# A fifth attention visit with float32 softmax weights, in an instruction order planned from new cost figures

## The chip, the cores and the metric

The kernel runs on one core of one Trainium2 chip. The metric is the device time of one execution in microseconds (us). Three executions of the kernel before took 832.07, 832.44 and 832.96 us; the median is 832.44 us.

## The reference

Hash-bucketed attention for 4 batches of 8 heads, 768 positions of 64 values each, then a two-layer network over the 3072 positions:

```
q_bits, k_bits = (q @ proj > 0), (k @ proj > 0)           # 6 bits: a bucket of 64
mask    = q_bucket == k_bucket
scores  = where(mask, q @ k.T / 8, -1e9)
attn    = softmax(scores)                                  # exp, sum, divide
x       = (attn @ v), heads side by side: 3072 x 512
h       = relu(x @ w_in)                                   # 512 -> 2048
out     = (h * h) @ w_out                                  # 2048 -> 512
```

Everything is float32 at the edges. The kernel gets float32 accuracy from float16 operands by carrying a high and a low half of each number and summing three products.

## The kernel before, in words

**Visits and units.** Attention is cut into 32 visits: one batch, one pair of heads, one half (384) of the queries. A visit has six units: 128 queries of one head against all 768 keys. Batch 0 is visited half by half (`WHOLE`): visits 0 to 3 are the four head pairs on half 0, visits 4 to 7 the same pairs on half 1. The other batches alternate halves pair by pair.

**A unit** (`unit`, L739): TensorE (PE) makes scores into a PSUM tile `pS` in four matmuls, `pS<-A,Q` and `pS<-L,M`; VectorE (DVE) scales them into `e` and finds the maximum; ScalarE (ACT) takes the exponential with its sum; `rv` is the reciprocal of that sum. From here there are two ways:

- the usual way: ACT writes `hl<-e,rv`, the high float16 half of the weights, DVE writes the low half, and SyncE (SP) issues one DMA transpose `aT<-hl`;
- the plain way (`PLAIN_AV`, visits 0 to 3): GpSimd (POOL) multiplies `e` by `rv` in float32, PE transposes it in six pieces `pT`, and ACT or DVE copies each group of three into `aT`. The units below 24 (`EARLY`) use the PSUM tiles `pm` and `pA` for this in turn, later ones a single tile, `misc`.

**The value product of a visit** (`av`, L783) is 36 pairwise float16 matmuls `pA<-aT,VV` the usual way, after V was split into halves, and 12 float32 ones `pA<-aT,V` the plain way, with V as loaded. ACT and DVE then write `xx`, two float16 halves.

**The network** (`moe`, L807) runs in eight stages, one per batch and half, when the four `xx` of that half are there. A stage has 16 steps: 12 matmuls `pm<-xx,win` of 384 columns; ACT and DVE make `g` from them (relu, square, high half, low half); then 9 matmuls `po<-wo,g` of 512 columns, three for each of the three 128-row blocks t. At the end of a stage ACT copies each block out, `o<-po`, and SP stores it. The three blocks lie in three banks of one PSUM tile `po`. The weights `win` and `wo` are split into halves from raw loads in the first fifth of the run: `top<-raw` on ACT, `f<-raw,top` on DVE, `win<-f` and `wo<-f`.

**Checks.** Near the end, `verify` (L882) reads q, k and v again (`X`) and the weights, and makes one flag; a general version of the program stands behind it and is not run with this input.

**What sets the order.** Nothing is issued in the order of the source. `Program.add` records every operation with its dependencies and a cost (`cost`, L195); `forward` (L318) lists them engine by engine against a model of the queues; `backward` refines the priorities; `emit` issues the best order found. So a change of a cost figure moves instructions on all five engines. Each engine then runs its list strictly in that order on the chip. `PACE` ties network steps to units so that PE has network matmuls to run while the attention units wait for the other engines. `region` (L156) says which part of a tile an operation touches: for PSUM it gave single banks, and it held two reads of one bank in order as well.

Of the kernel before, what the change touches and what calls it, by code (L numbers as in the profile page):

```python
# [23 lines left out]
P = 128  # L24
B, H, S, D = 4, 8, 768, 64
NB = 6
HS = 384
# [26 lines left out]
PLAIN_AV, DIVIDE = (0, 1, 2, 3), ("pool",)  # L54

WHOLE = {0: 0}

# [6 lines left out]
RUN = 18  # L64
CONSTS_BY, WIDE = ("sp", "sp", "sp"), 1
# [16 lines left out]
TRANSPOSES = 165  # L82
# [47 lines left out]
class Program:  # L130
# [25 lines left out]
    def region(view):  # L156
# [5 lines left out]
        if rec.kind == "psum":  # L162
            return 0, 1, f0 // 512, 1 + (f0 % rec.row + size(ap.ap[1:]) - 1) // 512, 0, 0, 0
# [5 lines left out]
    def add(self, *ways):  # L169
# [10 lines left out]
        for rec, w, (p0, p1, f0, f1, fs, g0, g1) in used:  # L180
            if rec.before is not None:
                deps |= rec.before.ops
            for j, w2, (a0, a1, b0, b1, bs, c0, c1) in rec.accesses:
                if (w or w2 or rec.kind == "psum") and a0 < p1 and p0 < a1 and b0 < f1 and f0 < b1 and not (fs and fs == bs and (c1 <= g0 or g1 <= c0)):
                    deps.add(j)
# [9 lines left out]
    def cost(key, name, args, kw):  # L195
# [16 lines left out]
        if name.startswith("dma"):  # L212
# [3 lines left out]
            return busy, b / (TRANSPOSES if name == "dma_start_transpose" else 314)  # L216
        if key == "act":
            t = 93 * (isinstance(kw.get("scale"), View) + isinstance(kw.get("bias"), View)) + (51 if "psum" in kinds[:2] else 93) + n / 1.2 + 93 * ("accum_out" in kw)
        elif key == "pool":
            t = 147 + n * (2.1 if args[0].dtype == F32 or args[0].dtype == F32R else 1.88) if name == "tensor_tensor" else 161 + n / 1.2 + 83 * ptr  # L220
        else:
            fast = name in ("tensor_copy", "tensor_scalar") and "psum" not in kinds[:2]
            both = len(args) > 3 and isinstance(args[3], View) and args[3].shape[-1] == 1
            t = 67 + 100 * ("accum_out" in kw) + n / (1.92 if fast else 0.96) + 62 * (ptr and (fast or name == "scalar_tensor_tensor")) + 100 * both
# [93 lines left out]
    def forward(self, prio, near):  # L318
# [7 lines left out]
        free = dict.fromkeys(keys, 0.0)  # L326
        out, dma, dge, held, kind = [], 0.0, 0.0, 0.0, None
# [11 lines left out]
        while True:  # L339
# [21 lines left out]
            if way[5] and held > t and (ready[k] or later[k] and later[k][0][0] < held):  # L361
                heapq.heappush(later[k], (held, i))
                continue
            ends = {}
# [84 lines left out]
def run(ctx: ExitStack, tc, kq, v, proj2, w_in, w_out, consts, out, flag):  # L449
# [56 lines left out]
    if fast:  # L506
# [8 lines left out]
        codes = sb([P, 4 * P], BF16, "codes")  # L515
# [148 lines left out]
    def first(hp):  # L664

        K, G = [sb([P, n], F32, name, tag="VV") for name, n in (("K", S), ("G", HS))]
# [3 lines left out]
        MK, MG = sb([P, S], F16, "MK", tag="M"), sb([P, HS], F16, "MG", tag="Q")  # L670
        halves = K[:, 0:HS], K[:, HS:], G
        pd = ps([P, 512], F32, "pd", tag="misc")[:, 0:HS]
        matmuls(*[(pd[32 * n : 32 * n + 32], pj, x) for n, x in enumerate(halves)])
        bits = sb([P, HS], BF16, "bits")
        act.activation(bits[0:96], pd[0:96], AF.Sign, scale=2.0**60, bias=thr[0:96])
        pc = ps([P, 3, 512], F32, "pc", tag="po")[:, :, 0:HS]
        for n in range(3):
            pe.matmul(pc[:, n], codes[0:96, n * P : (n + 1) * P], bits[0:96], start=True, stop=True)
        for n in range(2):
            dve.tensor_scalar(MK[:, n * HS : (n + 1) * HS], pc[:, n], 3 * 2.0**16, -65504.0, ALU.subtract, ALU.max)  # L680
        pr.add((act, "activation", (MG, pc[:, 2], AF.Relu), {"bias": shift}), (dve, "tensor_scalar", (MG, pc[:, 2], 2.0**16, 0.0, ALU.subtract, ALU.max), {}))
        return K, G, MK, MG

    def side_by_side(st, half, i):

        K, G, MK, MG = st
        c0 = half * HS + i * P
# [51 lines left out]
    def unit(st, half, i, aT, plain, pS=None):  # L739
        c0 = half * HS + i * P  # L740
# [42 lines left out]
    def av(b, hp, half, VV, aTs):  # L783
        pA = ps([P, 512], F32, "pA")[:, 0:HS]
# [8 lines left out]
        xx = xxs[b, half, hp] = sb([P, 2, HS], F16, "xx")  # L793
# [13 lines left out]
    def moe(n, b, half):  # L807
        X = [xxs.pop((b, half, cc)) for cc in range(NCC)]
# [5 lines left out]
        for f in range(NF + 1):  # L814
            if f == NF // 2:
                pr.checked = len(pr.ops)
            if f < NF:
# [3 lines left out]
                for cc in reversed(range(NCC)):  # L821
                    pr.mark = pace()
                    wh = win[:, 0, cc, f * P : (f + 1) * P]
                    wl = win[:, 1, cc, f * P : (f + 1) * P]
                    pe.matmul(pm[:, 0:HS], wh, X[cc][:, 0], start=cc == NCC - 1, stop=False)
                    pe.matmul(pm[:, 0:HS], wh, X[cc][:, 1], start=False, stop=False)
                    pe.matmul(pm[:, 0:HS], wl, X[cc][:, 0], start=False, stop=cc == 0)
                pr.rank, pr.mark = RANK_MOE, None

                g32 = sb([P, HS], F32, "g32", 2)  # L830
                pr.add((act, "activation", (g32, pm[:, 0:HS], AF.Relu), {"scale": HS2 if fast else 2.0**-23}),
                       (dve, "tensor_scalar", (g32, pm[:, 0:HS], HS2 if fast else 2.0**-23, 0.0, ALU.mult, ALU.max), {}))
                square(g32, g32)
                g = gs[f] = sb([P, 2, HS], F16, "g")
# [3 lines left out]
            if f > 0:  # L838
# [4 lines left out]
                if first:  # L843
                    po = ps([P, 3, DM], F32, "po")
                for t in range(3):
# [3 lines left out]
                    pe.matmul(po[:, t], gh, wo[:, 0, m], start=first, stop=False)  # L849
                    pe.matmul(po[:, t], gh, wo[:, 1, m], start=False, stop=False)  # L850
                    pe.matmul(po[:, t], gl, wo[:, 0, m], start=False, stop=last)
# [6 lines left out]
                for t in range(3):  # L858
                    r0 = b * S + half * HS + t * P
# [173 lines left out]
```

## Time and profile before

| | |
|---|---|
| median of three executions | 832.44 us |
| the profiled execution | 834.86 us, of which the span of instructions is 833.1 us |
| PE busy | 794.3 us (95%) |
| ACT busy | 656.6 us (79%) |
| DVE busy | 605.2 us (73%) |
| POOL busy | 72.7 us (9%) |
| DMA queue | 77.2% of 16 engines over the span, 144.93 MB |
| idle filler matmuls at the start | 67 |

A busy PE in this table counts matmuls from start to modelled end, and they overlap, so a stretch in which PE is called busy can still hold lost time. The useful reading is by stage: how much of a stretch PE idles, and what ended the idle time. A stage of the network is easy to find in the trace: its steps repeat `pm` and `po`.

### The profile page before, as it was taken

To read this page: it belongs to the slowest core of one execution; us is meant where nothing else is said; L and a number is where in the kernel's file an instruction comes from. 1 tells how busy PE (TensorE), PEld (TensorE's weight loads), DVE (VectorE), ACT (ScalarE), POOL (GpSimd) and SP (SyncE) were. 2 spreads that over 40 slices of the span, in tenths; PEclk is the share of its full clock that TensorE was granted. 3 is DMA by queue.
4 is the path that set the end of the run, shared out by engine and by line. 5 is a ranking of instruction groups with operands and counts; after the bars stand their busy time and mean duration, and the time that the engine had idled before them with its cause. 6 is when DMAs were issued, how large, how long until landed. Compare 5 with 4: busy or idle time off the path is not lost. (4 is left out here: it accounts for less than half of the span.)

```text
span 833.1 us, 14383 instructions
## 1 busy us (share of the span) xinstructions
PE 794.3 (95%) x5001; PEld 430.0 (52%) x5001; DVE 605.2 (73%) x1200; ACT 656.6 (79%) x1238; POOL 72.7 (9%) x175
## 2 busy tenths in 40 slices
PE   7797799999999999999999999999999999999996
PEld 4354355555555554555555545555555554555553
DVE  6888989998999888898879755888889433611110
ACT  5898999998888989888898856888988997334443
POOL 1255200100000010000000000000002000000000
PEclk9999999999999999999999999999999999999999
DMA  8985979999999999999989866988975889501001
GB/s 258 270 223 181 292 188 179 214 176 195 183 202 196 195 188 213 192 181 219 194 188 186 212 165 140 181 143 148 146 133 99 239 290 304 212 1 39 1 1 42
DMA packets 299521, 145.93 MB, mean 175 GB/s; under 512 B 268752, under 2 KB 279344, under 8 KB 299440
## 3 DMA queue, kind: packets, MB, share of 16 engines
q1 hardware_dynamic: 299440, 144.93, 77.2%
q8 instruction: 41, 0.67, 0.3%
q14 instruction: 40, 0.33, 0.1%
HBM read 56.80 MB, written 6.29 MB: 76 GB/s over the span
## 5 line engine op out<-in xcount | busy, mean ns | idle before, releaser
L427 PE MATMUL po<-wo,g 128*128 128x512 f16 x1152 | 296.9, 379 | 5.7 <-ACT o L427 5.7
L427 PE MATMUL pm<-xx,win 128*128 128x384 f16 x1536 | 297.7, 326 | 4.4 <-ACT g L427 2.8
L427 PEld LDWEIGHTS <-win 128*128 128x128 f16 x1536 | 149.9, 98 | 116.6 <-issue 8.0
L427 DVE TENSOR_SCALAR_CACHE_REDUCE e<-pS 128x768 f32<-128x768 f32 x192 | 182.7, 953 | 21.9 <-PE pS L427 17.7
L427 ACT ACTIVATE e<-e,maxes 128x768 f32<-128x768 f32 x192 | 178.2, 929 | 20.7 <-DVE e L427 19.2
L427 DVE SCALAR_TENSOR_TENSOR hl<-e,rv,hl 128x768 f16<-128x768 f32 x168 | 171.0, 1019 | 18.8 <-ACT hl L427 17.8
L427 PEld LDWEIGHTS <-g 128*128 128x128 f16 x1152 | 111.9, 98 | 124.8 <-issue 9.1
L427 ACT ACTIVATE hl<-e,rv 128x768 f16<-128x768 f32 x168 | 154.6, 923 | 6.0 <-DMA aT<-hl 5.2
L427 DVE SCALAR_TENSOR_TENSOR g<-g,g 128x384 f16<-128x384 f32 x121 | 66.9, 553 | 111.8 <-ACT g L427 111.4
L427 ACT ACTIVATE g<-g 128x384 f32<-128x384 f32 (+1 forms) x251 | 129.4, 517 | 6.6 <-PE po L427 2.7
L427 ACT ACTIVATE g<-pm 128x384 f32<-128x384 f32 x127 | 61.2, 482 | 90.3 <-PE pm L427 90.0
L427 PE MATMUL pS<-A,Q 128*128 128x384 f16 x372 | 93.1, 330 | 4.1 <-DVE e L427 2.6
L427 PE MATMUL pS<-L,M 128*128 128x384 f16 x372 | 91.8, 327 | 0.8 <-DMA M<-Q 0.8
L424 PE MATMUL pA<-aT,VV 128*64 128x384 f16 x1008 | 87.2, 327 | 0.0
L427 POOL TENSOR_SCALAR rv<-sums 128x1 f32<-128x1 f32 x136 | 36.8, 271 | 541.7 <-ACT e L427 400.2
L424 PEld LDWEIGHTS <-VV 128*64 128x64 f16 x1008 | 54.7, 110 | 32.9 <-issue 10.0
L427 PEld LDWEIGHTS <-Q 128*128 128x128 f16 x372 | 34.2, 98 | 43.1 <-issue 16.2
L427 DVE TENSOR_SCALAR M<-pc,masks 128x384 f16<-128x384 f32 x64 | 43.0, 672 | 15.4 <-PE pc L427 15.2
L427 PEld LDWEIGHTS <-M 128*128 128x128 f16 x372 | 36.3, 98 | 25.1 <-DMA M<-Q 1.2
L427 ACT ACTIVATION_READ_ACCUMULATOR e<-e,maxes 128x1 f32 x192 | 36.6, 191 | 0.0
L427 DVE SCALAR_TENSOR_TENSOR L<-R,A 128x768 f16<-128x768 f32 x32 | 30.4, 950 | 7.7 <-ACT A L427 7.5
L427 PE MATMUL pT<-unit_f,e 128*128 128x128 f32 x144 | 23.8, 293 | 10.5 <-ACT aT L427 7.7
(82 smaller groups left out, 517.4 us busy)
## 6 DMA issues: line engine op xcount, KB each, us to landing
R<-kq SPq DMA_DIRECT2D x32, 384.0 KB, 3.8
X<-kq SPq DMA_DIRECT2D x32, 384.0 KB, 4.1
raw<-w_in SPq DMA_DIRECT2D x16, 511.8 KB, 5.6
raw<-w_out SPq DMA_DIRECT2D x16, 511.8 KB, 4.9
V<-vp SPq DMA_DIRECT2D x20, 384.0 KB, 5.1
out<-o SPq DMA_DIRECT2D x24, 256.0 KB, 2.7
X<-vp SPq DMA_DIRECT2D x16, 384.0 KB, 4.4
Q<-L SPq DMA_DIRECT2D x32, 96.0 KB, 2.9
```

The source lines that it names most:

```text
L424: ins = q.engine.matmul(*map(real, args), **kw).ins
L427: ins = getattr(q.engine, o.name)(*map(real, o.args), **{k: real(x) for k, x in o.kw.items()}).ins
```

## The change

Five things are changed together.

1. `PLAIN_AV` gets a fifth visit, visit 4 (batch 0, first head pair, half 1). Its V is the float32 one that visit 0 loaded.
2. The cost figures of the planner are refitted: DMA loads, transposes, their landing and the time that the queue is held; a limit of eight transfers in flight (`LANES`) and of the backlog (`AT_MOST`); faster copies on DVE; slower strided copies on ACT; cheaper side-by-side matmuls.
3. `region` treats a PSUM tile as one piece, and two reads of it are no longer held in order in the plan.
4. In the last stage of the network the three blocks are not in `po`: t = 0 and 1 lie in the scores' tile `pS`, t = 2 in `pA`. In every stage the copy-out of t = 1 goes to DVE.
5. `codes` shares a buffer with `g32`, and half sizes become parameters, with the same values.

```diff
-PLAIN_AV, DIVIDE = (0, 1, 2, 3), ("pool",)
+PLAIN_AV, DIVIDE = (0, 1, 2, 3, 4), ("pool",)
-TRANSPOSES = 165
+TRANSPOSES, INSIDE, LOADING = 190, 230, 325
+SETUP, LANDING, TURNED, HOLD = 100, 1350, 500, 150
+AT_MOST = 2500
+LANES = 8
...
         if rec.kind == "psum":
-            return 0, 1, f0 // 512, 1 + (f0 % rec.row + size(ap.ap[1:]) - 1) // 512, 0, 0, 0
+            return 0, 1, 0, 1, 0, 0, 0
...
-                if (w or w2 or rec.kind == "psum") and a0 < p1 and ...
+                if (w or w2) and a0 < p1 and ...
...
+                if k != "pool":
+                    lanes.append(t + done)
+                    if len(lanes) >= LANES:
+                        busy = max(busy, lanes[-LANES] + 60 - t)
...
                 if first:
-                    po = ps([P, 3, DM], F32, "po")
+                    if fast and (b, q0 + nq) == (B - 1, S):
+                        po = ps([P, 2, 512], F32, "pS"), ps([P, 512], F32, "pA")
+                        po = [po[0][:, 0], po[0][:, 1], po[1]]
+                    else:
+                        po = ps([P, 3, DM], F32, "po")
+                        po = [po[:, t] for t in range(3)]
...
-                        move(o, po[:, t], back)
+                        move(o, po[t], back, (dve,) if fast and t == 1 else (act, dve, pool))
```

Three places in the new order matter for the prediction. The first is PE's list at the very end of the program, with the semaphores that a row waits for. Before:

```order
L427 MATMUL po<-wo,g 128x512
L427 LDWEIGHTS g
L427 MATMUL po<-wo,g 128x512 [waits Activation_49]
L427 LDWEIGHTS g
L427 MATMUL po<-wo,g 128x512
L427 LDWEIGHTS g
L427 MATMUL po<-wo,g 128x512
L427 LDWEIGHTS g
L427 MATMUL po<-wo,g 128x512 [waits Activation_49]
L427 LDWEIGHTS g
L427 MATMUL po<-wo,g 128x512
```

Now:

```order
L445 MATMUL pS<-wo,g 128x512
L445 LDWEIGHTS g
L445 MATMUL pA<-wo,g 128x512
L445 LDWEIGHTS g
L445 MATMUL pA<-wo,g 128x512
L445 LDWEIGHTS g
L445 MATMUL pA<-wo,g 128x512
L445 LDWEIGHTS g
L445 MATMUL pA<-wo,g 128x512
L445 LDWEIGHTS g
L445 MATMUL pA<-wo,g 128x512
```

The two waits for ScalarE between the last five matmuls are gone. Over the whole program 14 `po` rows waited for ScalarE before, at the ends and the starts of stages; in the new order six first rows of stages 2 to 7 wait for an engine that copies out, and none inside a stage. Between the last `po` row of stages 1 to 6 and that waiting row stand 57, 25, 17, 56, 15 and 16 other matmuls; the last stage's first rows wait for no copy-out.

The second place is ACT's list up to the fourth `xx<-pA`, the last input of the first network stage. `top`, `win` and `wo` are the splitting of weights, `aT` and `e,sums` belong to units. Before:

```order
L427 ACTIVATE top_87<-raw 128x512
L427 ACTIVATE aT<-pT 128x3x128 x2
L427 ACTIVATE wo<-f 128x512
L427 ACTIVATE aT<-pT 128x3x128
L427 ACTIVATE e,sums<-e,maxes 128x768
L427 ACTIVATE top_84<-raw 128x512
L427 ACTIVATE wo<-f 128x512
L427 ACTIVATE e,sums<-e,maxes 128x768
L427 ACTIVATE top_87<-raw 128x512
L427 ACTIVATE win<-f 128x512 x2
L427 ACTIVATE xx<-pA 128x384
```

Now:

```order
L445 ACTIVATE top_86<-raw 128x512
L445 ACTIVATE aT<-pT 128x3x128 x2
L445 ACTIVATE e,sums<-e,maxes 128x768
L445 ACTIVATE top_83<-raw 128x512
L445 ACTIVATE aT<-pT 128x3x128
L445 ACTIVATE e,sums<-e,maxes 128x768
L445 ACTIVATE top_86<-raw 128x512
L445 ACTIVATE win<-f 128x512
L445 ACTIVATE e,sums<-e,maxes 128x768
L445 ACTIVATE wo<-f 128x512
L445 ACTIVATE xx<-pA 128x384
```

Counted from the start of the program to that `xx` row, ACT's list had 22 `top`, 13 `win`, 8 `wo`, 26 `e,sums`, 46 `aT`, 7 `A` and 2 `VV` operations, and now has 17, 11, 4, 28, 49, 8 and 1. Weight splitting moved behind it, unit work in front of it. Further on, up to the exponential of the first unit of visit 7, ACT's list had 46 `aT`, 9 `A`, 5 `bits`, 32 `g`, 16 `hl`, 32 `top`, 15 `win`, 16 `wo` and 6 `xx` operations, and now has 60, 12, 6, 29, 11, 31, 12, 13 and 5.

The third place is PE's list where the first network matmuls stand. `pA<-aT,V` is the value product of visit 3, `pT` are float32 transposes. Before:

```order
L427 MATMUL pS<-L,M 128x384
L424 MATMUL pA<-aT,V 64x384 x12
L427 LDWEIGHTS win
L427 MATMUL pm<-xx,win 128x384
L427 LDWEIGHTS Q
L427 MATMUL pS<-A,Q 128x384
L427 LDWEIGHTS Q
L427 MATMUL pS<-A,Q 128x384
```

Now:

```order
L445 MATMUL pS<-L,M 128x384
L445 LDWEIGHTS win
L445 MATMUL pm<-xx,win 128x384
L445 MATMUL pT<-unit_f,e 128x128 x3
L445 LDWEIGHTS win
L445 MATMUL pm<-xx,win 128x384
L445 LDWEIGHTS win
L445 MATMUL pm<-xx,win 128x384
```

The transposes of visit 4 now stand between network matmuls, in groups of three. Before the first `pm` row PE's list holds 46 instead of 42 each of `pS<-A,Q` and `pS<-L,M` (two more units) and 150 instead of 144 transposes; the other 30 transposes of visit 4 come after it.

One count from farther on is used as well. Between the last scores of visit 20 and its value product PE's list had 36 `pm`, 27 `po`, 24 `pS`, 36 `pA<-aT,VV` and 2 `pc` matmuls; now it has 24 `pm`, 26 `po`, 24 `pS`, 4 `pd` and 1 `pc`. Visits 10, 17 and 18 changed in the same way, most other visits less. The 32 squares of `X` on ACT stood behind the `g<-pm` of network steps 88 to 95 of 128; now they stand behind those of steps 95 to 106, seven of them in a row at the first, where stage 7 begins.

More of the change, by code (lines that the diff above doesn't have):

```diff
@@ L325, in forward @@
         ready = {k: [] for k in keys}
-        free = dict.fromkeys(keys, 0.0)
-        out, dma, dge, held, kind = [], 0.0, 0.0, 0.0, None
+        free = dict.fromkeys(keys, 750.0)
+        out, rings, dge, held, kind, lanes = [], [0.0, 0.0], 0.0, 0.0, None, []
         def offer(i):
@@ L363, in forward @@
                 continue
+            if way[1].startswith("dma") and rings[int(k == "pool")] > t + AT_MOST:
+                heapq.heappush(later[k], (rings[int(k == "pool")] - AT_MOST, i))
+                continue
             ends = {}
@@ L736, in values, with unit @@
         return VV
-    def unit(st, half, i, aT, plain, pS=None):
-        c0 = half * HS + i * P
+    def unit(st, c0, i, aT, plain, pS=None):
         u = pr.rank
@@ L805, in unscaled, with moe @@
         return back
-    def moe(n, b, half):
-        X = [xxs.pop((b, half, cc)) for cc in range(NCC)]
+    def moe(n, b, q0, nq):
+        X = [xxs.pop((b, q0, cc)) for cc in range(NCC)]
         po, gs = None, {}
@@ L848, in moe @@
                     pr.rank, pr.mark = RANK_PE, pace()
-                    pe.matmul(po[:, t], gh, wo[:, 0, m], start=first, stop=False)
-                    pe.matmul(po[:, t], gh, wo[:, 1, m], start=False, stop=False)
-                    pe.matmul(po[:, t], gl, wo[:, 0, m], start=False, stop=last)
+                    pe.matmul(po[t], gh, wo[:, 0, m], start=first, stop=False)
+                    pe.matmul(po[t], gh, wo[:, 1, m], start=False, stop=False)
+                    pe.matmul(po[t], gl, wo[:, 0, m], start=False, stop=last)
                     pr.mark = None
@@ L926, in run, with pace @@
     step = [0]
-    def pace():
+    def pace(size=1):
         m = step[0]
-        step[0] += 1
+        step[0] += size
         for (u0, m0), (u1, m1) in zip(PACE, PACE[1:]):
@@ L945, in run @@
         F = WHOLE.get(b, H // 2) if fast else H // 2
-        visits += [(b, hp, half) for hp in range(F) for half in range(2)] + [(b, hp, 0) for hp in range(F, H // 2)] + [(b, hp, 1) for hp in range(F, H // 2)]
+        sizes = PARTS.get(b, (HS, HS)) if fast else (HS, HS)
+        parts = [(sum(sizes[:n]), x) for n, x in enumerate(sizes)]
+        visits += [(b, hp, *x) for hp in range(F) for x in parts] + [(b, hp, *x) for x in parts for hp in range(F, H // 2)]
     kept, kept_v = {}, {}
@@ L952, in ready @@
     def ready(visit, rank):
-        b, hp, _ = visits[visit]
+        b, hp, _, nq = visits[visit]
         if fast and visit < WIDE:
             pr.rank = rank
-            wide[visit] = first(hp)
+            wide[visit] = first(hp, nq)
         elif (b, hp) not in kept or not alive(x for st in kept[b, hp] for ab in st for x in ab):
@@ L966, in run @@
     done, u, stages = {}, 0, 0
-    for n, (b, hp, half) in enumerate(visits):
+    for n, (b, hp, q0, nq) in enumerate(visits):
         plain = fast and n in PLAIN_AV
-        aTs = [sb([P, KC, HS], F32, "aT") if plain else sb([P, 2 * KC, HS], F16, "aT") for _ in range(2)]
+        aTs = [sb([P, KC, nq], F32, "aT") if plain else sb([P, 2 * KC, nq], F16, "aT") for _ in range(2)]
         if n in wide:
-            for i in range(3):
-                for aT, pS in zip(aTs, side_by_side(wide[n], half, i)):
+            for i in range(nq // P):
+                for aT, pS in zip(aTs, side_by_side(wide[n], q0 + i * P, i)):
                     pr.rank = u
-                    unit(None, half, i, aT, plain, pS)
+                    unit(None, q0 + i * P, i, aT, plain, pS)
                     u += 1
@@ L977, in run @@
             for aT, st in zip(aTs, kept[b, hp]):
-                for i in range(3):
+                for i in range(nq // P):
                     pr.rank = u
-                    unit(st, half, i, aT, plain)
+                    unit(st, q0 + i * P, i, aT, plain)
                     u += 1
@@ L987, in run @@
         pr.rank = u - 0.5
-        av(b, hp, half, kept_v[b, hp, plain], aTs)
+        av(b, hp, q0, nq, kept_v[b, hp, plain], aTs)
         if n in early:
@@ L991, in run @@
             do(j)
-        done[b, half] = done.get((b, half), 0) + 1
-        if done[b, half] == H // 2:
-            moe(stages, b, half)
+        done[b, q0] = done.get((b, q0), 0) + 1
+        if done[b, q0] == H // 2:
+            moe(stages, b, q0, nq)
             stages += 1
```

82 lines of the change are left out of this document (45 added, 37 removed).

## The prediction

> **What bounds the kernel now.** I read the head of the page first, then busy time by stage, then the chain of waits, then the timeline where PE idles. The page's head, and the sums by stage (columns: stretch, its length, busy time and count of PE, PEld, DVE, ACT, POOL, then granted clock, DMA share, GB/s):
>
> ```profile
> span 833.1 us, 14383 instructions
> PE 794.3 (95%) x5001; PEld 430.0 (52%) x5001; DVE 605.2 (73%) x1200; ACT 656.6 (79%) x1238; POOL 72.7 (9%) x175
> ```
>
> ```profile
> 0.00:98.00 98.00, 74.95 (x485) 43.43 (x486) 79.90 (x177) 80.92 (x162) 36.09 (x53) 0.97 0.83 242
> 98.00:150.00 52.00, 50.28 (x300) 26.63 (x299) 48.10 (x97) 50.13 (x95) 5.37 (x13) 1.00 0.86 196
> 150.00:650.00 500.00, 496.05 (x3262) 269.78 (x3261) 428.46 (x843) 426.94 (x777) 31.28 (x109) 1.00 0.90 178
> 650.00:700.00 50.00, 48.10 (x273) 24.88 (x272) 15.14 (x33) 47.10 (x108) 0.00 (x0) 1.00 0.92 285
> 700.00:820.00 120.00, 119.31 (x664) 62.94 (x661) 32.85 (x54) 48.17 (x95) 0.00 (x0) 1.00 0.19 65
> 820.00:833.10 13.10, 5.61 (x26) 2.33 (x24) 0.73 (x2) 3.33 (x6) 0.00 (x0) 0.85 0.18 66
> ```
>
> From 150 us to 820 us PE idles 6.5 us in 670. There the time is PE's own work, and only less work or fewer stops on PE shorten it. In the first 98 us PE idles 23 us and ACT works 80.9 of 98 us; between 98 and 150 us ACT works 50.1 of 52. There ACT sets the pace. The timeline shows what ends this opening: the value product of visit 3, then ACT's `xx`, then the first network matmul.
>
> ```profile
> 92.57 4.09 PE L424 MATMUL pA<-aT,V 128*64 128x384 f32 x24 [0.33 <-DVE aT L427]
> 97.70 0.32 PE L427 MATMUL pm<-xx,win 128*128 128x384 f16 x1 [1.04 <-ACT xx L427]
> ```
>
> In the long middle one kind of stop repeats. In the list of waits (total, times, longest) it is this row, and the timeline at the end of stage 1 shows how it looks:
>
> ```profile
> PE po L427 <- ACT o L427: 5.7, 8, 0.9
> ```
>
> ```profile
> 199.38 0.81 PE L427 MATMUL po<-wo,g 128*128 128x512 f16 x3
> 200.88 0.59 PE L427 MATMUL po<-wo,g 128*128 128x512 f16 x2 [0.69 <-ACT o L427]
> ```
>
> The first block is complete, ACT copies it out, and PE's next matmul, into another bank of the same tile, waits until that copy is done. The end of the program has it twice in a row, in front of nothing else:
>
> ```profile
> 820.81 3.40 PE L427 MATMUL po<-wo,g 128*128 128x512 f16 x15
> ...
> 824.25 0.60 ACT L427 ACTIVATE o<-po 128x512 f32<-128x512 f32 x1 [1.64 <-PE po L427]
> ...
> 824.90 0.81 PE L427 MATMUL po<-wo,g 128*128 128x512 f16 x3 [0.69 <-ACT o L427]
> ...
> 825.74 0.60 ACT L427 ACTIVATE o<-po 128x512 f32<-128x512 f32 x1 [0.90 <-PE po L427]
> 826.39 0.59 PE L427 MATMUL po<-wo,g 128*128 128x512 f16 x2 [0.69 <-ACT o L427]
> ...
> 827.02 0.60 ACT L427 ACTIVATE o<-po 128x512 f32<-128x512 f32 x1 [0.68 <-PE po L427]
> ```
>
> **The change part by part.** The sum is made against the profiled span, 833.1 us. That execution took 834.86 us in all, 2.4 above the median of 832.44, so I carry only the difference over to the median. Rates come from the chain that ended last, where PE streams without a stop: 0.163 us for a `pm` matmul, 0.216 for a `po`, 0.163 for a score.
>
> ```profile
> 628.92 0.65 PE pS L427 x4
> 740.64 1.63 PE pm L427 x10
> 743.02 1.51 PE po L427 x7
> ```
>
> *The end, −1.7 us.* The last five matmuls need no copy-out now. Fifteen end at 824.21 (820.81 + 3.40); five more stream in 1.08 and end at 825.29; the last copy takes 0.60 and starts about 0.04 later, so it ends at 825.93 and not at 827.62 (827.02 + 0.60). The other two copies run meanwhile, one on DVE, and end before it. The store and what follows stay. I see 0.3 us of doubt either way.
>
> *Six ends of stages, −4.2 us.* Two of the eight stops are those of the end. The other six idle 5.7 − 2 × 0.69 = 4.3 us. From start to start it is more: the third matmul of 199.38 starts at 199.81, the next at 200.88, 1.07 instead of 0.216, so 0.85 lost, and 5.1 for six. The new order has no such wait inside a stage, but six first rows of stages wait for all three copies, which now go ACT, DVE, ACT, each behind the one before: about 0.6 each, 2 us with the handing over. In front of the waiting row stand 57, 25, 17, 56, 15 and 16 matmuls, 2.4 us or more. Three places have next to no reserve for a copy that stands behind other work on DVE, and behind DVE then waits ACT, with the `g` of the next step queued on it. I take 0.3 us for each of the three: −5.1 + 0.9. Bounds −5.1 and −2.
>
> *The fifth plain visit on PE, +5.7 us.* Rows for its parts (two from the whole run by form, one from a stretch of the timeline):
>
> ```profile
> L427 PE MATMUL pT<-unit_f,e 128*128 128x128 f32 x144 | 23.8, 293 | 10.5 <-ACT aT L427 7.7 <-POOL e L427 2.5
> 18.08 0.87 PE L427 MATMUL pT<-unit_f,e 128*128 128x128 f32 x6
> 424.63 3.12 PE L424 MATMUL pA<-aT,VV 128*64 128x384 f16 x36
> ```
>
> The value product goes from 3.12 to 4.09 us, +1.0. The 36 transposes cost between (0.87 − 0.29) / 5 = 0.116 us each in a row of six and 23.8 / 144 = 0.165 each over the run, so 4.2 to 5.9. I take 4.7, nearer the dense row, since most of them now stand between other matmuls that hide their ends. Bounds of the sum 5.2 and 6.9. The Trainium skill, FP8 and Floating Point Precision, section TensorE Precision Notes, says that true float32 takes four passes through the array. Four passes over 128 columns would be 4 × 0.163 / 3 = 0.217 us a transpose, 7.8 for 36, and the sum below would come out 3.1 us higher. The value product agrees with four passes (12 float32 pairs in 4.09 us against 36 float16 pairs in 3.12: 3.9 to 1), the transposes, at 0.116, do not.
>
> *The opening, −3.7 us.* ACT's durations up to the first network matmul (count, busy, mean ns):
>
> ```profile
> L427 ACT ACTIVATE e<-e,maxes 128x768 f32<-128x768 f32 x26 | 24.3, 936 | 0.8 <-DVE e L427 0.7
> L427 ACT ACTIVATE aT<-pT 128x384 f32<-128x384 f32 x46 | 20.7, 484 | 2.6 <-PE pT L427 2.4
> L427 ACT ACTIVATE top<-raw 128x512 f16<-128x512 bf16 x23 | 18.0, 782 | 3.9 <-DMA raw<-w_out 2.0 <-DMA raw<-w_in 1.5
> L427 ACT ACTIVATE win<-f 128x512 f16<-128x512 f32 x13 | 8.0, 619 | 0.3 <-DVE f L427 0.3
> L427 ACT ACTIVATE A<-R 128x768 f16<-128x768 f32 x7 | 5.9, 841 | 4.6 <-DMA R<-kq 4.6
> L427 ACT ACTIVATE wo<-f 128x512 f16<-128x512 f32 x8 | 5.0, 624 | 0.0
> ```
>
> Ahead of the fourth `xx` ACT's list loses 5 `top` (3.9), 2 `win` (1.2), 4 `wo` (2.5) and 1 `VV` (0.8, as an `A`) and gains 2 `e` (1.9), 3 `aT` (at 20.7 / 46 = 0.45, 1.4) and 1 `A` (0.8): −4.3 us. So the first network matmul should come about 4.3 us earlier, and PE has by then two units' scores (8 matmuls, 1.3) and six transposes (0.7) more behind it: 6.3 us less lost. What was put off comes back in the ACT-bound stretch that follows. Up to the exponential of the first unit of visit 7 ACT's list gains 14 `aT` (6.3), 3 `A` (2.5) and a `bits` (0.6), and loses 5 `hl`, 1 `top`, 3 `win`, 3 `wo`, 3 `g` and an `xx`; the last two kinds take 0.5 each, an `hl` 0.92:
>
> ```profile
> L427 ACT ACTIVATE hl<-e,rv 128x768 f16<-128x768 f32 x168 | 154.6, 923 | 6.0 <-DMA aT<-hl 5.2
> L427 ACT ACTIVATE g<-g 128x384 f32<-128x384 f32 x127 | 65.8, 518 | 2.1
> ```
>
> That is 9.4 − (4.6 + 0.8 + 1.9 + 1.9 + 1.5 + 0.5) = −1.8. Of the lead of 4.3 some 2.5 is spent again, so 6.3 − 2.5 = 3.8 stays; I write 3.7. Bounds: −6.3, if ACT's idle time (17 us of the first 98) absorbs what was put off, and 0, if the opening hangs on loads and on PE's own queue. DVE's list loses 6 low halves of `hl` there as well, so DVE does not take ACT's place. The six DMA transposes and one load of V that go count for nothing: ACT's rows above wait for loads of `R` and of raw weights, none for a transpose or for V.
>
> *The checks, −0.7 us.* Between 650 and 700 us PE idles 1.9 us, 0.7 of it a stage end counted above. The squares are spread over twelve network steps instead of eight, but seven stand in a row at the first, 5.9 us by an `A` of the same size. Bounds −1.2 and +2.
>
> *Value products closer to their scores, 0.* The timeline and the DMA view for visit 20:
>
> ```profile
> 404.84 0.96 DVE L427 TENSOR_SCALAR_CACHE_REDUCE e<-pS 128x768 f32<-128x768 f32 x1
> 416.33 1.45 SPq L427 DMA_TRANSPOSE aT<-hl  x1
> aT<-hl SPq DMA_TRANSPOSE x168, 3.9
> ```
>
> From scores to landing it took 416.33 + 3.9 − 404.84 = 15.4 us, and PE came at 424.63. In the new list PE has 24 `pm`, 26 `po`, 24 `pS`, 4 `pd` and 1 `pc`, some 14 us, to hide it. The new lists also bring the last unit's work forward on ACT and DVE. I take no cost; the bound is four visits at 1 us.
>
> The sum: −1.7 − 4.2 + 5.7 − 3.7 − 0.7 = −4.6. The span comes to 828.5 us, the median to 827.8.
>
> **The rivals.**
>
> *The transposes hold up PE's queue: slower.* After the first network matmul come ten groups of three transposes in PE's list, each waiting for POOL's product and for the one tile `misc`, which ACT must have emptied, while ACT is the busiest engine. Everything behind waits, network matmuls too. For it: PE idled 10.5 us in front of `pT`, 7.7 of it for ACT. Against: that was in the opening, with little else to run, and with groups close together. Take the opening's gain away (+3.7) and let ten groups wait 0.6 us each: −4.6 + 3.7 + 6 = +5.1, about 837.5. It decides as soon as lost gain and waits pass 4.6 us together.
>
> *The opening keeps all its gain.* ACT had 17 us idle there. With −6.3 instead of −3.7 the time is 825.2; a further 3 us of ACT's idle time gone gives 822.
>
> *The stops at the ends of stages only move.* If the chain ACT, DVE, ACT is late at all six ends, PE waits there as long as before: −4.6 + 4.2, no change, 832.0. The short cover at three of them speaks for it, the 56 and 57 matmuls at two against.
>
> *The order is too tight.* Four value products wait 1 us and the seven squares cost 2: −4.6 + 4 + 2.7 = +2.1, 834.5; with half of that, 831.2.
>
> **How the numbers follow.** The forecast has 0.57, the full opening 0.17, the held queue 0.10, the moved stops 0.08, the tight order 0.08. Within 0.2% is within 1.7 us, about what a measurement of this kernel can tell from no change, so faster means below 830.8. Faster then takes the forecast without its upper edge (0.54), the full opening and a little of the others: 0.78. Within 0.2%: the moved stops and parts of forecast and tight order, 0.11. Slower: 0.11. For the range I let the forecast's own ends stand at 823 and 832, by its bounds, reach down to 821.5 for the full opening and up to 833 for the moved stops and half the tight order; the held queue stays outside.
>
> **What would show it.** Right: no PE idle time put down to ACT's `o` inside a stage or at the end; last copy about 0.6 us behind PE's last matmul; the first `pm` at 92 to 95 us; PE busy in network steps from there. Wrong: a first `pm` after 97 us, PE idle in front of `pT` by more than 5 us between 90 and 130 us, PE idle in front of `pA<-aT,VV` at visits 10, 17, 18 or 20, or ACT standing for DVE's `o` with `g` behind it.

## The result, and the profile after

After takes **821.32 us** (median of four executions: 818.54, 820.10, 822.53 and 1683.85 us; the last is left out of every comparison, and nothing like it came back in five more executions). Before took 832.49 us beside it. The ratio is 0.9855, interval 0.9824 to 0.9885, so after is 11 to 12 us faster. The five (e9 below) gave 822.5 us and 0.9865 (0.9843 to 0.9886). The forecast was 827.8 with a range from 821.5 to 833.0: the sign was right, the size two fifths of what came, and the result lies 0.2 us below the range's lower edge.

The profiled execution of after took 820.10 us. Its head, and the sums by stage (columns as before: length, busy time and count of PE, PEld, DVE, ACT, POOL, then granted clock, DMA share, GB/s):

```profile
span 818.2 us, 14399 instructions
PE 797.2 (97%) x5043; PEld 433.2 (53%) x5043; DVE 599.3 (73%) x1226; ACT 648.0 (79%) x1235; POOL 90.2 (11%) x156
```

```profile
0.00:98.00 98.00, 86.00 (x577) 51.01 (x578) 83.81 (x197) 85.66 (x178) 44.61 (x57) 1.00 0.77 235
98.00:150.00 52.00, 52.00 (x320) 27.52 (x319) 49.76 (x99) 50.65 (x96) 8.16 (x14) 1.00 0.93 218
150.00:450.00 300.00, 298.66 (x1994) 162.78 (x1993) 275.16 (x577) 271.00 (x494) 29.57 (x68) 1.00 1.03 206
450.00:650.00 200.00, 199.13 (x1252) 107.24 (x1250) 137.59 (x260) 141.33 (x261) 7.85 (x18) 1.00 0.61 120
650.00:700.00 50.00, 50.00 (x293) 26.55 (x292) 18.62 (x43) 41.77 (x89) 0.00 (x0) 1.00 0.64 180
```

The span fell by 14.9 us (833.1 − 818.2), PE's busy time rose by 2.9 (797.2 − 794.3), so PE idles 17.8 us less. By stage: 11.0 less in the first 98 us (98 − 86.00 = 12.0, was 98 − 74.95 = 23.05), 1.7 less up to 150, 1.9 less between 650 and 700 (50.00 of 50), the remaining 3.2 in the other stretches. So three fifths of the idle time that went (11.0 of 17.8) lay in the opening, to which the forecast gave 3.7 of its 10.3 us of gains. Of the 14.9 us, 3 to 4 belong to the two executions and not to the kernels: the profiled one of before was 2.4 above its median, that of after 1.2 below.

PE's two longest waits for ACT in the opening, before and then after (a row of waits: total, times, longest):

```profile
PE pT L427 <- ACT aT L427: 7.7, 8, 2.2
PE pc L427 <- ACT bits L427: 3.0, 2, 2.8
```

```profile
PE pT L445 <- ACT aT L445: 1.1, 3, 0.5
PE pc L445 <- ACT bits L445: 0.2, 1, 0.2
```

They are 9.4 us shorter together, most of the 11.0.

The opening ends the same way as before, 9.3 us earlier (was 97.70). PE's timeline:

```profile
83.29 4.09 PE L442 MATMUL pA<-aT,V 128*64 128x384 f32 x24
...
88.37 0.32 PE L445 MATMUL pm<-xx,win 128*128 128x384 f16 x1
88.84 0.52 PE L445 MATMUL pT<-unit_f,e 128*128 128x128 f32 x3
89.19 0.98 PE L445 MATMUL pm<-xx,win 128*128 128x384 f16 x5
90.01 0.49 PE L445 MATMUL pT<-unit_f,e 128*128 128x128 f32 x3
```

The transposes of the fifth visit stand between the network matmuls, and no row has idle time in front. ACT's sum and its waits up to the first `pm`, before and then after:

```profile
0.00:97.70 97.70, 74.65 (x485) 43.33 (x485) 79.60 (x175) 80.62 (x162) 36.09 (x53) 0.97 0.83 242
```

```profile
ACT A L427 <- DMA R<-kq: 4.6, 2, 3.0
ACT bits L427 <- PE pd L424: 3.5, 2, 3.3
ACT aT L427 <- PE pT L427: 2.4, 3, 1.5
ACT top L427 <- DMA raw<-w_out: 2.0, 2, 1.6
ACT top L427 <- DMA raw<-w_in: 1.5, 3, 0.6
```

```profile
0.00:88.40 88.40, 76.55 (x517) 44.81 (x517) 74.23 (x175) 76.08 (x158) 40.65 (x53) 1.00 0.78 237
```

```profile
ACT bits L445 <- PE pd L442: 7.1, 2, 6.8
ACT L445 <- DVE masks L445: 1.6, 1, 1.6
ACT aT L445 <- PE pT L445: 1.1, 1, 1.1
```

ACT's fourth number is its busy time: 80.62 became 76.08, 4.5 us less. Its idle time went from 17.1 (97.7 − 80.62) to 12.3 us (88.4 − 76.08), 4.8 less. The 8.1 us of waits for loads are all gone, but not all of that is gained: the wait for `pd` (PE's product from which ACT makes `bits`, the signs for the buckets), at the start of the program, grew from 3.5 to 7.1. Before, ACT waited 3.01 us for its first load and then 3.32 for `pd`; after, it waits 6.78 for `pd` at once, and starts that `bits` at 9.61 us instead of 9.20.

The end of the program, from PE's last matmuls (the last copy starts 0.04 us behind the last of them, 810.12 + 1.24):

```profile
810.12 1.24 PE L445 MATMUL pA<-wo,g 128*128 128x512 f16 x5
810.32 0.60 ACT L445 ACTIVATE o<-pS 128x512 f32<-128x512 f32 x1 [2.01 <-PE pS L445]
810.95 0.69 DVE L445 TENSOR_SCALAR o<-pS 128x512 f32<-128x512 f32 x1 [2.04 <-ACT o L445]
811.40 0.60 ACT L445 ACTIVATE o<-pA 128x512 f32<-128x512 f32 x1 [0.48 <-PE pA L445]
```

All of PE's waits from 100 us on that are named:

```profile
PE pS L445 <- DVE e L445: 1.6, 3, 0.8
PE po L445 <- ACT o L445: 0.2, 1, 0.2
PE po L445 <- ACT g L445: 0.2, 1, 0.2
```

The eight stops for ACT's `o`, 5.7 us, are down to one of 0.2.

### The profile page after: what moved, and what is told of

Read it like the earlier page. It is cut to its first block, busy times and chain, and to the rows that moved or that the text cites. A ratio compares the mean times of both kernels' runs of the same rounds, so it can differ in the third digit from the quotient of the medians.

```text
span 818.2 us, 14399 instructions
## 1 busy us (share of the span) xinstructions
PE 797.2 (97%) x5043; PEld 433.2 (53%) x5043; DVE 599.3 (73%) x1226; ACT 648.0 (79%) x1235; POOL 90.2 (11%) x156
## 4 chain that ended last, share of the span: by engine, by line
PE 83%; ACT 8%; DVE 4%; issue 2%; DMA 2%; POOL 0%; ACTq 0%; DVEq 0%
PE pm L445 28%; PE po L445 24%; PE pS L445 14%; PE pA L442 10%; ACT e L445 2%; DMA aT<-hl 2%; ACT aT L445 2%; PE pd L442 2%; PE pA L445 1%; DVE e L445 1%; ACT hl L445 1%; PE pT L445 1%; DVE hl L445 1%; PE pc L445 1%; PE idle L438 1%
## 5 line engine op out<-in xcount | busy, mean ns | idle before, releaser
L445 PE MATMUL pm<-xx,win 128*128 128x384 f16 x1536 | 305.6, 326 | 0.0
L445 PE MATMUL po<-wo,g 128*128 128x512 f16 x1008 | 278.6, 380 | 0.6 <-ACT o L445 0.2
L445 DVE SCALAR_TENSOR_TENSOR hl<-e,rv,hl 128x768 f16<-128x768 f32 x162 | 165.3, 1024 | 24.4 <-ACT hl L445 23.6
L445 ACT ACTIVATE hl<-e,rv 128x768 f16<-128x768 f32 x162 | 149.6, 926 | 18.4 <-DMA aT<-hl 14.1
L445 DVE SCALAR_TENSOR_TENSOR g<-g,g 128x384 f16<-128x384 f32 x115 | 63.8, 555 | 116.8 <-ACT g L445 107.8
L445 PE MATMUL pS<-L,M 128*128 128x384 f16 x372 | 94.2, 326 | 0.0
L442 PE MATMUL pA<-aT,VV 128*64 128x384 f16 x972 | 84.2, 328 | 0.0
L445 POOL TENSOR_SCALAR rv<-sums 128x1 f32<-128x1 f32 x100 | 32.7, 327 | 455.4 <-ACT e L445 390.0
L445 PEld LDWEIGHTS <-Q 128*128 128x128 f16 x372 | 34.5, 98 | 37.3 <-issue 12.3
L445 PE MATMUL pS<-wo,g 128*128 128x512 f16 x96 | 34.9, 379 | 0.0
L445 POOL TENSOR_SCALAR e<-e,rv 128x768 f32<-128x768 f32 x30 | 32.9, 1100 | 16.9 <-DVE rv L445 9.7
```

Of the source, the lines that this page charges most:

```text
L442: ins = q.engine.matmul(*map(real, args), **kw).ins
L445: ins = getattr(q.engine, o.name)(*map(real, o.args), **{k: real(x) for k, x in o.kw.items()}).ins
```

## The experiments

The opening gave more than was forecast, so the question is which part of the change did that, and whether it is the part or the order that happened to come out. Two theories were set against each other first. **F**: the refitted figures carry the opening, because with them ACT no longer waits for a load. **V**: the fifth visit carries it. Below, "ends" means the new rule for PSUM tiles, the last stage outside `po`, and the copy of t = 1 on DVE. The column us is (ratio − 1) × 832.4, so a gain is negative, and the idle columns are the lengths of a stretch less PE's busy time in it, from the sums by stage. Rates are the planner's `TRANSPOSES, INSIDE, LOADING`.

| kernel | figures | plain visits | ends | ratio (interval) | us | PE idle 0 to 98 | 150 to 450 |
|---|---|---|---|---|---|---|---|
| before | old | 4 | old | 1 | 0 | 23.0 | 2.6 |
| e13 | old, transposes 163 | 4 | old | 1.0036 (1.0017, 1.0055) | +3.0 | 23.0 | 4.3 |
| e14 | old, transposes 168 | 4 | old | 1.0004 (0.9988, 1.0020) | +0.3 | 20.9 | 1.4 |
| e2 | old | 5 | old | 0.9996 (0.9976, 1.0015) | −0.3 | 16.5 | 1.0 |
| e4 | new | 4 | old | 0.9974 (0.9957, 0.9992) | −2.2 | 16.5 | 0.8 |
| e5 | old | 4 | new | 0.9948 (0.9934, 0.9963) | −4.3 | 17.7 | 1.5 |
| e6 | new | 5 | old | 0.9962 (0.9949, 0.9975) | −3.2 | 14.7 | 4.5 |
| e3 | old | 5 | new | 0.9963 (0.9944, 0.9982) | −3.1 | 17.3 | 1.0 |
| e1 | new | 4 | new | 0.9922 (0.9893, 0.9950) | −6.5 | 17.3 | 2.2 |
| after | new | 5 | new | 0.9855 (0.9824, 0.9885) | −12.1 | 12.0 | 1.3 |
| e9, after again | new | 5 | new | 0.9865 (0.9843, 0.9886) | −11.2 | 11.7 | 0.9 |
| e15 | 191, 231, 326 | 5 | new | 0.9875 (0.9847, 0.9902) | −10.4 | 13.3 | 1.6 |
| e16 | landing 1400 | 5 | new | 0.9861 (0.9832, 0.9889) | −11.6 | 13.6 | 0.8 |
| e8 | 185, 225, 320 | 5 | new | 0.9895 (0.9880, 0.9909) | −8.7 | 14.8 | 0.3 |
| e17 | 185, 225, 320 | 4 | new | 0.9904 (0.9875, 0.9933) | −8.0 | 15.9 | 0.2 |
| e10 | 195, 235, 330 | 5 | new | 0.9991 (0.9973, 1.0009) | −0.7 | 14.9 | 7.0 |
| e18 | 195, 235, 330 | 4 | new | 1.0016 (0.9996, 1.0036) | +1.3 | 16.5 | 8.2 |
| e11 | new, no limits | 5 | new | 0.9997 (0.9982, 1.0013) | −0.2 | 17.8 | 2.6 |
| e7 | new | 5 | old PSUM rule | 0.9982 (0.9964, 0.9999) | −1.5 | 13.5 | 1.3 |
| e12 | new | 6 | new | 0.9931 (0.9911, 0.9951) | −5.7 | 11.3 | 2.7 |

The ratios rest on 3 to 12 executions of a kernel, the idle columns on one each. Single executions of one kernel differ by up to 8 us (before: 829.81 to 836.63 in one set; e7: 827.64 to 835.96), so a span from one trace is not set against a median here.

### Taking the parts out of after, one at a time

**Without the fifth visit** (e1).

```
-PLAIN_AV, DIVIDE = (0, 1, 2, 3, 4), ("pool",)
+PLAIN_AV, DIVIDE = (0, 1, 2, 3), ("pool",)
```

> The changed kernel with four plain visits again, all else as changed. Theory F (the refitted figures of loads and queues carry the opening: they order loads so that ACT no longer waits for them): first network matmul at 87 to 91 us, time 818 to 824 us, since PE loses 5 us of work and ACT gets 6 high halves back. Theory V (the fifth visit carries it, by taking the halves and transposes of six units away): first network matmul at 94 us or later, 827 to 831 us.

**With the old figures** (e3): `cost`, and the queue model in `forward`, as in before.

```
-TRANSPOSES, INSIDE, LOADING = 190, 230, 325
+TRANSPOSES, INSIDE, LOADING = 165, 230, 325
...
-            return busy, b / TRANSPOSES if name == "dma_start_transpose" else SETUP + b / (INSIDE if inside else LOADING)
+            return busy, b / (TRANSPOSES if name == "dma_start_transpose" else 314)
```

> The changed kernel planned with the old cost figures and the old queue model; fifth visit, PSUM rule and last stage as changed. Theory F: first network matmul at 95 us or later; the stops at the ends of stages stay away, so 826 to 831 us. Theory V: 819 to 823 us, as the changed kernel.

Measured: 827.2 us without the visit, where V has it, and 829.69 with the old figures, where F has it. Both lose, and both lose part of the opening: PE idles 17.3 us of the first 98 in either, where after has 12.0. The first `pm` comes at 91.1 and 91.9 us, earlier than V (94) and F (95) said. Neither theory holds alone.

### Putting the parts into before, one at a time and in a pair

**The fifth visit alone** (e2) and **the figures alone** (e4; with them `cost` and the queue model in `forward`, as in after).

```
-PLAIN_AV, DIVIDE = (0, 1, 2, 3), ("pool",)
+PLAIN_AV, DIVIDE = (0, 1, 2, 3, 4), ("pool",)
```

> The kernel before with the fifth plain visit alone, old figures and old rules. Theory F: first network matmul still at 95 us or later, ACT still waits 6 us or more for loads there, time 831 to 837 us (PE has 5 us more work). Theory V: first network matmul at 88 to 91 us, 822 to 826 us.

```
-TRANSPOSES = 165
+TRANSPOSES, INSIDE, LOADING = 190, 230, 325
+SETUP, LANDING, TURNED, HOLD = 100, 1350, 500, 150
+AT_MOST = 2500
+LANES = 8
...
```

> The kernel before planned with the new cost figures and queue model alone: four plain visits, old PSUM rule, old last stage. Theory F: first network matmul at 87 to 91 us, ACT's waits for loads under 2 us, the eight stops at ends of stages still there, 822 to 827 us. Theory V: first network matmul at 95 us or later, 830 to 834 us.

Measured: 832.47, in F's range though the first `pm` comes at 92.0 us and not at 95, and 830.53, in V's range with the first `pm` at 96.0 as V has it. By sums up to 98 us, e2 and then e4:

```profile
0.00:98.00 98.00, 81.52 (x524) 46.04 (x525) 83.25 (x186) 86.37 (x177) 45.81 (x59) 0.98 0.81 240
```

```profile
0.00:98.00 98.00, 81.52 (x545) 46.92 (x546) 82.71 (x191) 85.19 (x171) 41.24 (x50) 0.98 0.86 254
```

PE works 81.52 us in both, 6.6 more than in before. The fifth visit brings nothing by itself, since PE has its work to do as well (+4.8 us or more, below); the figures bring a little. Less idle time in the opening is thus not time gained: each part alone takes 5.4 to 6.6 us of it (e2, e4, and e5 below), and they gain 0.3, 2.2 and 4.3 us. F fails on its own ground as well: with the figures alone ACT still waits for a load, in the list of its waits up to the first `pm` at 96.0 us:

```profile
ACT A L443 <- DMA R<-kq: 5.5, 2, 5.3
```

**The ends alone** (e5), **the figures and the visit** (e6). e5's edit is the third and fourth point of the change on before's figures, e6's is those of e2 and e4 together.

> Before, with only the new rule for PSUM tiles, the last stage in the scores' tile and the value product's tile, and the copy of t = 1 on DVE; four plain visits, old figures. By the prediction's own terms this holds the end (-1.7) and the six ends of stages (-4.2): about 826.5 against 832.4, first pm at 97 to 98 us as before, and no PE stop for ACT's o. If the three edits pay only together, as the runs so far suggest, less: 829 to 831, with the stops gone and the time back in other stops.

> Before with the refitted figures and the fifth visit, old rule for PSUM, old last stage. If parts add, figures (-1.8) and visit (0) give 830.5. If the figures are what lets the fifth visit pay (no ACT wait for loads at the start), the first pm comes at about 88 us and the time is after's plus the two terms of the ends, 821.3 + 5.9 = 827.

Measured: 829.15 and 830.5. The ends bring 4.3 us (3.1 to 5.5 by the interval), half to nine tenths of the 5.9 that the forecast gave them, as the second branch has it; PE's waits for ACT's `o` fall from 5.7 to 0.5 us over the run. The figures and the visit together bring 3.2, near their sum of 2.5, as the first branch has it. All three alone make −0.3 − 2.2 − 4.3 = −6.8 us, and after has −11.2 to −12.1: four to five us come only with all three. After also has the fifth point of the change, the shared buffer of `codes`, which none of e2, e4, e5 and e6 has and no run tests by itself. e1 has it, and its −6.5 is just the sum of figures and ends, so nothing speaks for a worth of its own.

**The old PSUM rule in after** (e7).

```
-            return 0, 1, 0, 1, 0, 0, 0
+            return 0, 1, f0 // 512, 1 + (f0 % rec.row + size(ap.ap[1:]) - 1) // 512, 0, 0, 0
...
-                if (w or w2) and a0 < p1 and ...
+                if (w or w2 or rec.kind == "psum") and a0 < p1 and ...
```

> After with only the old rule for PSUM tiles (single banks, two reads held in order) in the plan. If the stage ends are the rule's doing, PE stops for ACT's o come back at six stages, 0.85 us each: 826 against 821.3, with the opening as in after (first pm 88 us). If the opening hangs on the plan as a whole, the first pm moves by 3 us or more, and the time is 827 to 830.

Measured: 831.75 us, with executions from 827.64 to 835.96. That is 10 us over after, twice what the first branch expected. Stops at copies of `o` came back, five instead of six (1.7 us for ACT's, 1.6 for DVE's), and the opening stayed (13.5 us idle, first `pm` at 89.2). The profiled execution, 828.03, is the second lowest of twelve, and what the usual one loses further is not in a trace. That part stays open.

### Is it the order that was drawn?

Every changed figure gives another order of thousands of instructions, so 5 us could be the draw. Two theories were set against each other: **D**, any changed figure draws another order, and orders of one family spread by some 10 us; **S**, the edits carry the gain. Four neighbours of after's figures and two of before's were tried. e8, e10 and e15 move the three rates down by 5, up by 5, and up by 1:

```
-TRANSPOSES, INSIDE, LOADING = 190, 230, 325
+TRANSPOSES, INSIDE, LOADING = 185, 225, 320
```

> After with the three rates of transfers in the planner 2% lower (185, 225, 320), a change far below what the refit moved. If after's gain is a property of fitted figures, 820 to 823.5. If it is a lucky draw among orders of about equal worth, the time moves by more than 4 us, to 825 to 829, with another opening or other stops in the middle.

> After, unchanged, in more executions: 820 to 822.5 by both theories. Beside it stand the nudged plans, so that the worth of this one order among its neighbours is read on one chip.

> After with the three rates of transfers in the planner 2 to 3% higher (195, 235, 330). The downward nudge gave 0.9895 against 0.9855. If after is one draw out of a spread of some 4 us around a better level, this lies between 821 and 828. If its figures are the best fit and both sides lose, 823 to 826. First pm at 88 to 92 us either way.

> After with the three rates of transfers raised by 1 each (191, 231, 326), a third to a half per cent. D: 821 to 832, at no set distance from after's 822. S: 821 to 824, since nothing that the chip could show tells these figures from after's.

e16 has `LANDING` 1400 for 1350; e13 and e14 are before with `TRANSPOSES` 163 and 168 for 165.

> After with the planner's landing time of a load at 1400 instead of 1350 ns. D: 821 to 832. S: 821 to 824.

> Before with its planner's transposes at 163 instead of 165. Theory D (draw: any figure that changes draws another order, and orders of one family spread by some 10 us): anywhere from 826 to 838, and before is an ordinary member. Theory S (the edits carry the gain, before is what its family gives): 831 to 834.

> Before with its planner's transposes at 168 instead of 165. D: 826 to 838, not the same as the nudge down. S: 831 to 834.

Measured: 823.01 and 822.29 us for the two nearest neighbours of after, 824.77 for the nudge down, 831.4 for the nudge up; 835.65 and 832.82 for before's. The two nearest neighbours and e14 lie where S has them. Three runs miss: e13 lies 1.7 us above S's 831 to 834, e8 between its two ranges, and e10 above both of its own (821 to 828 and 823 to 826). Apart from the nudge up the two families don't meet: 821 to 825 against 832 to 836. So the gain does not hang on one order, and inside a family the spread is about 3 us. With the nudge up the spread of after's family is 10 us, as D has it, so D is not excluded. Against a mere draw speaks that the number of visits hardly moves it: with four (e18) the nudge up is as bad as with five (e10), and the nudge down as good with four (e17) as with five (e8).

> The kernel of e8 (rates 185, 225, 320) with four plain visits. With the fifth it took 824.8. The pair after and e1 gave 5.9 us for the fifth visit. If that is the visit's own worth, 830 to 831; if it was the draw, anywhere from 821 to 832.

> The kernel of e10 (rates 195, 235, 330) with four plain visits. With the fifth it took 831.4. If the fifth visit is worth 5.9 us by itself, 837; if it was the draw, 821 to 832, more likely lower than 831.

Measured: 824.3, in the range of the draw and far from the 830 to 831 of a fifth visit with a worth of its own, and 833.89, between the two. The traces show where the time goes. Waits between 150 and 450 us, where the sums by stage have the DMA share at 0.98 in before and 1.03 in after, for the two kernels with the lower rates (e8, e17) and then the two with the higher ones (e10, e18):

```profile
PE pS L445 <- DVE e L445: 0.2, 1, 0.2
ACT hl L445 <- DMA aT<-hl: 5.7, 9, 1.7
```

```profile
PE pS L445 <- DVE e L445: 0.2, 1, 0.2
ACT hl L445 <- DMA aT<-hl: 2.6, 5, 0.9
```

```profile
PE pS L445 <- DVE e L445: 4.2, 9, 1.7
ACT hl L445 <- DMA aT<-hl: 13.2, 14, 3.2
```

```profile
PE pS L445 <- DVE e L445: 6.1, 9, 1.1
PE pA L442 <- DMA aT<-hl: 1.2, 4, 0.6
ACT hl L445 <- DMA aT<-hl: 15.8, 19, 2.1
```

The longest of these in e10, in its timeline, reads from the queue to PE:

```profile
179.09 8.30 SPq L445 DMA_TRANSPOSE aT<-hl  x3
...
186.47 0.93 ACT L445 ACTIVATE hl<-e,rv 128x768 f16<-128x768 f32 x1 [3.22 <-DMA aT<-hl]
...
187.44 1.02 DVE L445 SCALAR_TENSOR_TENSOR hl<-e,rv,hl 128x768 f16<-128x768 f32 x1 [2.10 <-ACT hl L445]
...
188.37 0.95 DVE L445 TENSOR_SCALAR_CACHE_REDUCE e<-pS 128x768 f32<-128x768 f32 x1
...
189.39 0.48 PE L445 MATMUL pS<-A,Q 128*128 128x384 f16 x2 [1.68 <-DVE e L445]
```

Three transposes were planned close together and held the queue for 8.30 us. ACT's next `hl` writes a buffer that a transpose still reads, waits 3.22 us, DVE's low half waits behind it, then DVE's reading of the scores, then PE. With the rates 1.5 to 2.6% higher ACT waits like this fourteen and nineteen times, 13.2 and 15.8 us (in after ten times, 7.5 us), and PE idles 7.0 to 8.2 us in that stretch instead of 0.2 to 1.6. Against the lower rates that is most of the difference of 8 to 9 us. That the higher rate makes the planner pack the transposes closer is a reading of this; the three rates were not moved one by one.

### The limits on transfers, and a sixth visit

**Without the limits** (e11).

```
-LANES = 8
+LANES = 800
...
-AT_MOST = 2500
+AT_MOST = 2500000
```

> After without the planner's limits of eight transfers in flight and of the backlog (LANES 800, AT_MOST 2.5 million). If the limits carry the opening's gain (SP's list as it really drains), ACT waits for loads again, 3 us or more up to the first pm, which comes at 91 us or later: 825 to 828. If the refitted rates carry it, no more than another plan drawn: 820 to 826 with the first pm at 88 to 91.

Measured: 831.88 us, the whole gain lost, and more than either expectation had. The first `pm` comes at 93.3 us, PE idles 17.8 us of the first 98 instead of 12.0, and ACT waits for a load again, at the very start. ACT's timeline, and the same `bits` in after:

```profile
6.25 0.84 ACT L445 ACTIVATE A<-R 128x768 f16<-128x768 f32 x1 [4.22 <-DMA R<-kq]
9.11 0.58 ACT L445 ACTIVATE bits<-pd,masks 96x384 bf16<-96x384 f32 x1 [2.01 <-PE pd L442]
```

```profile
9.61 0.58 ACT L445 ACTIVATE bits<-pd,masks 96x384 bf16<-96x384 f32 x1 [6.78 <-PE pd L442]
```

So the limits are needed for the opening within the new figures, as the first branch of the expectation had it, but not through this wait: behind it ACT starts `bits` at 9.11 us, half a microsecond earlier than in after. Up to its first `pm` ACT works 3.1 us longer than in after (79.17 against 76.08) and idles 1.9 longer, at waits that come later. By the two traces the spans differ by 10.2 us: PE works 1.0 us longer, and idles 5.8 us longer in the opening, 1.2 between 150 and 450 and 2.4 from 700 us to the end of the span.

**A sixth plain visit** (e12): `PLAIN_AV` (0, 1, 2, 3, 4, 5).

> After with a sixth plain visit, visit 5. PE gets 5 us more work again. The fifth gave 5.5 us less PE idle time in the opening with either set of figures. If the sixth still finds idle time to fill, 820 to 822; if the opening is full by now (PE idles 12 of the first 98 us, and none from 98 to 150), its work comes on top: 825 to 827.

Measured: 827.49 us, half a microsecond above the second branch's range. PE idles 11.3 us of the first 98 (11.7 and 12.0 with five), so there is no more to fill, and the sixth visit's work comes on top. No kernel was measurably ahead of after.

## Why the prediction was right or wrong, point by point

**The end, −1.7, and six ends of stages, −4.2: right in kind, a little too large.** The last copy runs 0.04 us behind the last matmul as written, the stops inside a stage are gone, and the feared waits at the first rows of stages are 0.2 us. By themselves the two bring 4.3 us (e5), against −5.9.

**The fifth visit on PE, +5.7: right, with +4.8 to +5.8 measured.** The rows by form for the whole run of after:

```profile
L445 PE MATMUL pT<-unit_f,e 128*128 128x128 f32 x180 | 27.6, 279 | 4.9 <-POOL e L445 2.7 <-ACT aT L445 1.1 <-POOL rv L445 0.3
L442 PE MATMUL pA<-aT,V 128*64 128x384 f32 x120 | 20.5, 491 | 0.8 <-ACT aT L445 0.6
```

Against before the 36 transposes add 27.6 − 23.8 = 3.8 us, 0.106 each. But some of before's ran at half clock (last section). In e1, with four visits and the clock at 1.00 through the first 98 us, the 144 take 22.8 us, so 36 more add 4.8, 0.133 each, near the 4.7 taken and far below the 7.8 that four passes would make. The value product adds 20.5 / 5 − 3.12 = 1.0, as forecast.

**The opening, −3.7: the step that failed.** Its parts were a list of ACT's 4.3 us shorter, which came (4.5); a first `pm` earlier by just these 4.3 us, where 9.3 came, to 88.4 us and so ahead of the 92 to 95 named as a sign; 6.3 us less lost on PE; and 2.5 handed back up to visit 7. Instead PE idles 11.0 us less in the first 98 us, and another 1.7 less up to 150.

Two steps of it were wrong. The forecast held ACT's idle time of 17 us fixed, and kept it for a bound and a rival; it fell by 4.8 us, the other half of the 9.3. And the 2.5 us were counted by ACT's list alone, and nothing was handed back. In the twelve traces with a fifth visit (or a sixth) PE works 50.8 to 52.0 of the 52 us from 98 to 150, in the eight with four visits 48.4 to 50.4. So there the fifth visit gives PE work beside what ACT had put off.

Why ACT's idle time fell is not shown. The refit of the loads is the nearest reason, since before had 8.1 us of waits for them, but it does not go by these waits alone. With the old figures and the fifth visit they fall as well, to 2.6 us in e2 and 0.3 in e3. e1 and e3 have 0.3 us of them up to the first `pm`, and PE idles 17.3 us of the first 98, about as in e11 with 4.2 (17.8). e4 has 5.7, and ACT idles 12.2 us up to the first `pm`, as in after. Nor is an early first `pm` the gain by itself: e10 has it at 87.2 us and gains 0.7, e16 at 91.6 and gains 11.6.

**The checks, −0.7.** Between 650 and 700 us PE is never idle, 1.9 less than before; less the 0.7 of a stage end this is 1.2, the better bound. The row of squares costs nothing.

**Value products closer to their scores, 0: right.** PE waits nowhere in front of `pA<-aT,VV` in after. It does in e18 (1.2 us, four times), so the cover was thin, as the rival said.

**The rivals.** *Full opening* (0.17; 825.2 and down to 822 with 3 us of ACT's idle time gone) is the nearest: it had both steps, nothing handed back and ACT's idle time shorter, with 3 us where 4.8 went. *Transposes hold up PE's queue* (slower): no row of `pT` waits between 90 and 150 us; false. *The stops only move*: false by the 0.2 us. *The order too tight* did not come, but stood close by: rates 1.5 to 2.6% higher give 831.4 us. That this is close to the 831.2 that it gave for half its price is chance, since most of the stops stand in front of `pS` and not at the value product.

**What stays open.** Why ACT's idle time fell, what e7 loses beyond its 3.3 us of stops, and the four to five us that only all three parts together bring. A reading of the last that fits: each part takes another of PE's reasons to wait away, and while one is left, work that comes early waits at it. Idle time in the traces supports that only in the opening (16.5 to 17.7 with one part alone, 14.7 with the visit and the figures, 12.0 with the ends too). Against it stand the lower rates, at which four visits already gain 8.0 us (e17) and the fifth adds only 0.7 (e8); and the spread inside a family, about 3 us, is more than half of the sum in question.

## What to carry to other kernels

When a change redraws the order of instructions, don't hold the idle time of the pacing engine fixed. List it by what ended it, and ask of each wait what stands behind it: the wait for a load in e11 cost nothing, because the next one would have taken its place. Work that one engine's list puts off is handed back only if the other engines have nothing to do beside it. In these plans the slow side was the safer one for the planner's rates: 1.5 to 2.6% lower cost 3 us, and as much higher 10. And before a part is credited with a gain, take it out of two or three neighbouring plans: the fifth visit gained 4.7 to 5.6 us in one pair of plans, and between −1.2 and +2.1 in the five others.

## What the runs showed of the hardware

In before, PE runs at half its clock twice in the opening. Sums of its trace around the first place (the third number from the right is the granted clock):

```profile
25.60:30.60 5.00, 0.85 (x5) 0.31 (x3) 3.88 (x8) 3.41 (x7) 1.81 (x3) 0.98 0.99 212
30.60:33.80 3.20, 3.09 (x12) 2.13 (x13) 1.01 (x2) 1.73 (x6) 0.99 (x2) 0.50 0.83 227
```

and the second:

```profile
61.00:64.20 3.20, 1.45 (x11) 0.79 (x9) 2.62 (x5) 2.68 (x7) 1.31 (x2) 1.00 1.08 279
64.20:67.60 3.40, 3.28 (x15) 2.42 (x16) 2.25 (x6) 2.79 (x7) 1.35 (x2) 0.55 0.85 291
```

After 5 us in which PE worked 0.85, and after 3.2 in which it worked 1.45, it got half its clock for 3.2 to 3.4 us. The Trainium skill, TensorE: Matmul & The Clock Gate, Part 1, describes a monitor that drops PE to half its rate after an idle window of about 3.4 us and gives it back after a busy one; the first place agrees, and at the second the clock fell although PE had worked 1.45 of the 3.2 us. How much work keeps the clock is not shown: in e5 PE worked 1.39 us from 31.0 to 34.2, and the clock stayed at 1.00. In after no stretch of the first 98 us has a lower clock. Where the clock falls, a gap costs more than its length: by an estimate from these rows some 3.1 us (3.2 × 0.50 + 3.4 × 0.45) were lost in before while PE counted as busy, which is part of why PE's busy time rose by only 2.9 us in after. It is no large share of the gain: over 97 executions of before the mean granted clock went from 0.987 to 0.998, and the time followed it with a correlation of only −0.30.

The time between the last copy's end and the end of the span was no constant either: 5.5 us in before, 6.2 in after, and 8.1 in e8 and e4. e4 ends as before does and e8 as after does, so it is not the new end that makes the difference, and a single execution carries 2 to 3 us of it.
